# Efficient attention and a Fourier mixing block on one core: five steps set to other places in a hand-written order

## The chip, the cores and the metric

The kernel runs on one core of a Trainium2 chip. Its engines are TensorE (PE in the profile, with PEld for its weight loads), VectorE (DVE), ScalarE (ACT), GpSimd (POOL) and SyncE (SP, which here only issues DMAs). The metric is the device time of one execution in microseconds; a kernel is told by the median of several executions.

## The reference

Eight batches of 576 tokens with 8 heads of 64. Attention is linear: q is softmaxed over its 64 elements, k over the tokens, and q times (k transposed times v) is the result. Its output goes through a two-dimensional Fourier transform whose real part is added, a layer norm, and a feed-forward layer of 2048.

```python
q_s = softmax(q, axis=-1); k_s = softmax(k, axis=2)
kv  = einsum('bhsd,bhse->bhde', k_s, v)
x   = einsum('bhsd,bhde->bhse', q_s, kv)   # to (B, S, H*D)
u   = x + real(fft(fft(x, axis=1), axis=2))
un  = (u - mean(u)) / sqrt(var(u) + 1e-6)
out = u + relu(un @ w_ch1) @ w_ch2
```

## The kernel before

**Groups.** Each batch has 512 tokens of its own group, held as two tiles x of 128 partitions times two rows of 512; the remaining 64 tokens of all eight batches together make a ninth, shared group (xs). Nine groups of 512 tokens go one after the other ("orders" 0 to 8) through the feed-forward layer: groups 0 to 6, then the shared group (number 8), then group 7, the eighth batch.

**One order.** `up` multiplies the normalized and transposed tokens unT with the first weights, `down` the hidden values with the second. Both use Strassen's scheme with seven products in place of eight, with PSUM banks ba, bb and bc; DVE and ACT combine the products (L1141 and L1182 in `up` and in the `down` of order 1, L1304 in the later ones). A bank can't be written by the next product until DVE or ACT has read it. From order 2 on, six of the seven products of `down` are split once more by the same scheme (`deep_down`); the combinations of second weights that this needs are made once, in the `down` of order 1, by `deepen` (L1198): for each of six products two DVE subtractions and two POOL subtractions (L1206) and seven stores of 256 KB to the DRAM buffer w2d (L1212), three of them straight from the streamed weights at once and four from the results six units later. Weights stream from DRAM into four places of the buffer `big`; when the last matmul of a product has used one, `used` (L1194) issues the load of the one four further on (`load`, L449), on SP's queue.

**What else lies in an order.** While PE works on order n, the attention of batch n+1, its transform and its norm are done in between. `attention_timed` (L497) has four key blocks (load L579 and L592, maximum L620 on DVE, Exp L626 on ACT, transposition L644 and L652 on PE, copies L648 and L657, product with v L669) and four query blocks (load L696, maximum L723, Exp L729, transposition L750, product L803 with copy L812 or L814). In every second batch `t_times_kv` (L818) handles the shared tokens: four matmuls (L827), two ACT copies (L834, L835) and three DVE folds (L839 to L842), whose result the transform (`folded`, `block`, from L848 on) takes. `norm` (L996) has four statistics on DVE (L1005, L1006), a Sqrt on ACT (L1009), two small DVE operations (L1012, L1013), four normalizations on ACT (L1034), their transpositions on PE (L1040), copies on ACT (L1048) into unT, and `combine`, three DVE operations and one on POOL (L398 to L401). Its step `back` (L1016) is an Exp of one column on ACT (L1020): it makes the Exp table the active one again after the Sqrt. There is one buffer for unT, which the next group's copies can only fill when the last one has been read.

**The order is written out by hand.** Every step of orders 1 to 8 is a pair of a time and a function. `timed` (L1456) puts the pairs of one order together, they are sorted by time (a stable sort), and their instructions are issued in that sequence to the engines' queues. The times are units without a dimension: one unit is one step of PE in `up`, of four matmul instructions (eight in the `down` of order 1 are two units). So a time tells between which other instructions a step stands in each queue, and nothing more. `up` has 56 units, the `down` of order 1 has 56, the later ones 50. Every queue works its instructions in sequence, also SP's: a DMA that must wait keeps those behind it waiting.

**The stores of group 1** (`down`, function `out` at L1393, and `store`, L1406). Two of the four 256 KB pieces go straight to the output (L1418), two go to a DRAM buffer `mirror` (L1425), from which they are copied to the output with the columns of each head turned around (L1427) nine units later. They stand behind the last additions to x (L1396) on DVE.

Of the kernel before, what the change touches and what calls it, by code (L numbers as in the profile page):

```python
# [80 lines left out]
UP, TWICE = NP * len(ORDER), 8 + 6 * len(ORDER)  # L81
# [12 lines left out]
def at(t, script):  # L94
    return [(t + dt, step) for dt, step in script]
# [42 lines left out]
class _Block:  # L138
# [358 lines left out]
    def attention_timed(self, b, start, end):  # L497

        keys = [("k", b, r) for r in range(NR)]
        tail = [("t", b)] if b % 2 == 0 else []  # L500
        own = [("q", b, c, u) for c in range(2) for u in range(2)]
        first = start + 14 + 5 * len(tail)
        gap, steps = (end - 13.7 - first) / 3, []
        for i, it in enumerate(keys):
            t = start + 3.5 * i
            steps += at(t - 5.5, self.k_load(it)) + at(t, self.k_exp(it)) + at(t + 4, self.k_turn(it))
            steps += at(t + 7, self.k_times_v(it))
        for it in tail:
            t = start + 14
            steps += at(t - 12, self.t_load(it)) + at(t, self.q_exp(it)) + at(t + 8, self.t_turn(it))  # L510
            steps += at(21 if start < 0 else 35, self.t_fold(it))
        for i, it in enumerate(own):
            t = first + gap * i
            steps += at(t - 6.5, self.q_load(it)) + at(t, self.q_exp(it)) + at(t + 8.7, self.q_turn(it))
            steps += at(t + 11.7, self.q_times_kv(it))
        return steps + at((33 if start < 0 else 42) if tail else 22, self.t_times_kv(b))

    def second_keys(self):

# [476 lines left out]
    def norm(self, g):  # L996

        nc, V = self.nc, self.nc.vector
        mv = self.small.tile([P, 4, 2], F32, tag="mv", name="mv", bufs=2)
        std = self.small.tile([P, 4], F32, tag="std", name="std", bufs=2)  # L1000
        uns, box = {}, {}

        def stats(i):
            st = self.small.tile([P, 6], F32, tag="st", name="st", bufs=2)
            V.bn_stats(st[:], self.xpart(g, i % 2, i // 2))  # L1005
            V.bn_aggr(mv[:, i, :], st[:])  # L1006

        def root(s):
            nc.scalar.activation(std[:, s], mv[:, s, 1], ACT.Sqrt, bias=self.eps[:, 0:1])  # L1009

        def scales(s):
            V.reciprocal(std[:, s], std[:, s])  # L1012
            V.scalar_tensor_tensor(out=mv[:, s, 0], in0=mv[:, s, 0], scalar=-1.0, in1=std[:, s], op0=ALU.mult,  # L1013
                                   op1=ALU.mult)

        def back():  # L1016
            if g > 0:

                t = self.small.tile([P, 1], F32, tag="root", name="root", bufs=1)
                nc.scalar.activation(t[:], std[:, 0:1], ACT.Exp, scale=0.0)  # L1020

        def normal(i):
            un = self.halves()
            x = self.xpart(g, i % 2, i // 2)
            if g == 0:
                V.tensor_scalar(out=un[:, 0:D], in0=x, scalar1=std[:, i:i + 1], scalar2=mv[:, i, 0:1], op0=ALU.mult,
                                op1=ALU.add)
                if i == 0:
                    words = self.w2sb.rearrange("p f n -> p (f n)").rearrange("p (a n) -> p a n", n=2 * D)
                    self.gate(un[:], words[0:1, 1:4, 0:2])  # L1030
                if i == 1:
                    self.wait_for(un, [self.raws[i] for i in range(4, 11)])
            else:
                nc.scalar.activation(un[:, 0:D], x, ACT.Identity, bias=mv[:, i, 0:1], scale=std[:, i:i + 1])  # L1034
            uns[i] = un

        def turn(i):
            pt = self.turned()
            for k in range(KT):
                nc.tensor.transpose(pt[:, k, :], uns[i][:, k * P:(k + 1) * P], self.ident[:])  # L1040
            box[i] = pt

        def laid(i):
            if g not in self.unT:
                self.unT[g] = self.work.tile([P, 7, 2, HD], F32, tag="unT", name="unT", bufs=1)
            c, u = i % 2, i // 2
            cols = slice(c * P, (c + 1) * P)
            nc.scalar.copy(self.unT[g][:, u:u + 3:2, :, cols], box.pop(i)[:].rearrange("p (a k) t -> p a k t", a=2))  # L1048

        def combine():  # L1050
            if g > 0:
                unT = self.unT[g]
                self.b_side(lambda i: unT[:, i], lambda i: unT[:, i], V, nc.gpsimd, V)

        steps = []
        put = lambda t, f, *a: steps.append((t, lambda: f(*a)))
        if g == 0:
            for some in ((0, 2), (1, 3)):
                s = slice(some[0], 4, 2)
                for i in some:  # L1060
                    put(0, stats, i)
                for f in (root, scales):
                    put(0, f, s)
        else:
            for n, i in enumerate((0, 2, 1, 3)):
                put((0, 1, 4, 5)[n], stats, i)
            s = slice(0, 4)
            put(6.5, root, s)
            put(9, scales, s)
            put(16.5, back)  # L1070
        for n, i in enumerate((0, 2, 1, 3)):
            put(9.3 + 1.3 * n, normal, i)
            put(11.8 + 1.3 * n, turn, i)
            put(12.6 + 1.3 * n, laid, i)
        put(17.5, combine)
        return steps
# [286 lines left out]
    def down(self, g, order):  # L1363
        if order > 1:
            return self.deep_down(g, order)
        nc, V = self.nc, self.nc.vector
        h = [self.hpairs(p) for p in range(NP)]
        steps, t = [], 4 * 2
        for k, m in enumerate(ORDER):
            if m != 1:  # L1370
                spare = [self.hblock(A_AT[ORDER[k - 1]], a, b) for a in range(2) for b in range(2)]
                n = self.base[order] + NP + k
                steps += at(t * k, self.deepen(m, n, spare if k % 2 else [self.gap(i) for i in range(4)]))

        def product(m, bank, first):
            n = self.base[order] + NP + ORDER.index(m)

            def run(i, q):
                w = self.stream[n]
                for p in range(4 * q, 4 * q + 4):  # L1380
                    nc.tensor.matmul(bank()[:, i, :], lhsT=h[p][:, A_AT[m], i * P:(i + 1) * P], rhs=w[:, p, :],
                                     start=first and i == 0 and p == 0, stop=p == NP - 1,
                                     skip_group_check=True)
                if (i, q) == (1, 1):
                    self.used(n)
            return [lambda i=i, q=q: run(i, q) for i in range(2) for q in range(2)]

        def early(i, j, t):
            u, d = i - 1 if (i, j) != (1, 2) else 0, j - 1
            x = lambda: self.xs[g, u][:, :, d * HD:(d + 1) * HD]  # L1390
            return [(0, lambda: nc.gpsimd.tensor_tensor(out=x(), in0=x(), in1=t()[:], op=ALU.add))]

        def out(u, d, store):  # L1393
            def run(bank, t):
                x = lambda: self.xs[g, u][:, :, d * HD:(d + 1) * HD]
                steps = [(0, lambda: V.tensor_tensor(out=x(), in0=bank()[:], in1=x(), op=ALU.add))]  # L1396
                for c in range(2 * store):
                    steps += at(9 + c, self.store(g, c, u, lambda c=c: self.xpart(g, c, u)))
                return steps
            return run  # L1400


        return steps + self.strassen(product, 2, {(1, 1): out(0, 0, False), (2, 1): out(1, 0, True),
                                                  (2, 2): out(1, 1, False), (1, 2): out(0, 1, True)}, early)
# [26 lines left out]
def kernel(ctx: ExitStack, tc: tile.TileContext, q, kT, v, w1, w2, ft,  # L1431
                                                           cd, out):
    blk = _Block(ctx, tc, q, kT, v, w1, w2, ft, cd, out)
# [22 lines left out]
    def timed(t, order, g):  # L1456
        b = order + 1
        steps = at(t, blk.up(order, g)) + at(t + UP, blk.down(g, order))
        if order == B:
            return steps + [(t + 6 + 1.2 * i, lambda i=i: blk.later and blk.later.pop(0)()) for i in range(36)]  # L1460
        if b == B:
            return steps + at(t + UP + 29, blk.norm(groups[b]))
        start, end = -7 if order > 2 else 0, 45
        steps += at(t, blk.attention_timed(b, start, end)) + at(t + end, blk.folded(b))
        t += UP
# [30 lines left out]
    groups = [*range(B - 1), B, B - 1]  # L1496
# [8 lines left out]
    n = 2 * NF - 10  # L1505
# [20 lines left out]
    n = 0  # L1526
# [15 lines left out]
    t, steps = 0, []  # L1542
    for order, g in enumerate(groups[1:], 1):
        steps += timed(t, order, g)
        t += UP + (TWICE if order > 1 else UP)
# [58 lines left out]
```

## Time and profile before

| | us |
|---|---|
| median of 11 executions | 1115.88 (1113.9 to 1120.67) |
| the profiled execution | 1115.26 |
| its span in the profile | 1113.5 |
| mean granted clock of TensorE | 0.995 |
| `up` of order 1, by the timeline of PE | 193.5 to 257.6 |
| `down` of order 1 | 257.6 to 314.9 |
| `up` of order 2 | 314.9 to 384.1 |
| `down` of order 7 | 961.8 to 1009.8 |

The other busy shares are DVE 60%, POOL 45% and ACT 37%. The hidden layer's matmuls lie on lines L1171 (`up`), L1381 (`down` of order 1), L1267 and L1297 (`deep_down`); in all these rows a tile's name stands before its line, `out<-in`. A line of a timeline has the start, the duration, the engine, the line, the operation with its tiles, how often it occurs, and in brackets the idle time before it with what ended it. A line of the waits has who waited for whom, the total in us, the number of times and the longest.

### The profile page before, as it was taken

How to read it: one execution, taken by the hardware profiler on the slowest of the kernel's cores; microseconds unless marked ns; L12 is line 12 of the kernel's file. 1: busy time of each engine (PE TensorE's matmuls, PEld its weight loads, DVE VectorE, ACT ScalarE, POOL GpSimd, SP SyncE). 2: the span in 40 equal slices, each digit the busy share in tenths (PEclk: the TensorE clock that was granted, in tenths of full speed). 3: DMA queues.
4: the chain of work that ended last, by engine and by line, in shares of the span. 5: the costliest groups of instructions: out<-in, count | busy, mean ns of one | idle time of the engine just before them, and what ended most of it. 6: DMA issues, size and time to landing. Idle time of an engine off the chain costs nothing.

```text
span 1113.5 us, 16988 instructions
## 1 busy us (share of the span) xinstructions
PE 1060.7 (95%) x6336; PEld 917.1 (82%) x6336; DVE 664.1 (60%) x1313; ACT 413.4 (37%) x1001; POOL 498.4 (45%) x409
## 2 busy tenths in 40 slices
PE   5799989999989999999999999999999999999997
PEld 4644446888878899889988998889988998898896
DVE  6784795664646665667555775758456742563351
ACT  6694424452225314442344225521452132222200
POOL 1074671254513545256533841465436353554343
PEclk9999999999999999999999999999999999999999
DMA  9565686446986466636674567466654565575463
GB/s 307 180 225 179 249 293 223 155 156 224 316 284 210 150 235 222 222 142 235 237 259 150 202 242 225 157 223 229 233 201 152 188 239 178 197 264 188 166 238 122
DMA packets 114913, 236.41 MB, mean 212 GB/s; under 512 B 24320, under 2 KB 76288, under 8 KB 104208
## 3 DMA queue, kind: packets, MB, share of 16 engines
q1 hardware_dynamic: 113032, 234.29, 61.0%
q10 hardware_dynamic: 1800, 1.05, 0.3%
q8 instruction: 50, 0.82, 0.3%
q14 instruction: 31, 0.25, 0.1%
HBM read 200.18 MB, written 39.32 MB: 215 GB/s over the span
## 4 chain that ended last, share of the span: by engine, by line
PE 56%; DVE 7%; ACT 2%; issue 1%; DMA 1%; POOL 1%; SPq 0%; DVEq 0%; ACTq 0%; POOLq 0%
PE bb L1171 11%; PE bb L1297 8%; PE bc L1171 7%; PE ba L1171 7%; PE ba L1297 5%; PE bc L1297 5%; PE bb L1267 3%; DVE big L1243 2%; PE acc L669 2%; PE acc L803 1%; PE acc L951 1%; PE tr L1040 1%; PE acc L914 1%; PE acc L917 1%; DVE unT L401 1%
## 5 line engine op out<-in xcount | busy, mean ns | idle before, releaser
L1171 PE MATMUL bb<-unT,big 128*128 128x256 f32 x768 | 185.4, 381 | 8.7 <-DVE krec L631 4.1
L391 POOL TENSOR_TENSOR big<-big 128x512 f32<-128x512 f32 (+1 forms) x38 | 46.3, 1220 | 278.0 <-ACT big L1183 277.2
L1171 PEld LDWEIGHTS bb<-unT,big 128*128 128x128 f32 x768 | 142.8, 191 | 29.1 <-DVE krec L631 4.5
L1183 ACT ACTIVATE big<-big 128x512 f32<-128x512 f32 x96 | 60.4, 629 | 193.0 <-DVE big L1182 192.6
L1171 PE MATMUL ba<-unT,big 128*128 128x256 f32 x512 | 124.1, 379 | 0.2 <-ACT unT L1048 0.2
L1171 PE MATMUL bc<-unT,big 128*128 128x256 f32 x512 | 123.7, 379 | 0.0
L1297 PE MATMUL bb<-big 128*128 128x128 f32 x848 | 105.5, 276 | 3.2 <-DVE u L1304 3.2
L1141 DVE TENSOR_TENSOR u<-bb,s 128x512 f32<-128x512 f32 x66 | 45.5, 689 | 100.0 <-PE bb L1171 87.8
L1171 PEld LDWEIGHTS bc<-unT,big 128*128 128x128 f32 x512 | 94.6, 190 | 12.2 <-DVE big L1182 0.8
L1171 PEld LDWEIGHTS ba<-unT,big 128*128 128x128 f32 x512 | 94.4, 190 | 12.2 <-ACT unT L1048 0.5
L1297 PEld LDWEIGHTS bb<-big 128*128 128x128 f32 x848 | 99.6, 192 | 4.4 <-DVE u L1304 4.4
L1247 POOL TENSOR_TENSOR x<-x,big 128x512 f32<-128x512 f32 x52 | 77.4, 1498 | 35.9 <-DVE big L1304 18.4
L1243 DVE TENSOR_TENSOR big<-big 128x512 f32<-128x512 f32 x92 | 86.1, 979 | 5.9 <-POOL big L392 3.4
L1297 PE MATMUL ba<-big 128*128 128x128 f32 x640 | 79.7, 275 | 0.0
L1297 PEld LDWEIGHTS ba<-big 128*128 128x128 f32 x640 | 76.4, 192 | 1.2
L729 ACT ACTIVATE q<-q,qm 128x64 f32<-128x64 f32 x240 | 64.7, 338 | 30.8 <-DVE qm L723 23.8
L1243 POOL TENSOR_TENSOR big<-big 128x512 f32<-128x512 f32 x26 | 41.4, 1604 | 61.5 <-DVE big L1243 61.5
L1182 DVE TENSOR_TENSOR big<-bc,u 128x512 f32<-128x512 f32 x64 | 44.0, 688 | 23.6 <-PE bc L1171 22.5
L1304 DVE TENSOR_TENSOR u<-bb,s 128x256 f32<-128x256 f32 x40 | 16.8, 419 | 63.5 <-PE bb L1297 45.6
L1297 PE MATMUL bc<-big 128*128 128x128 f32 x416 | 51.7, 275 | 0.0
L1267 PE MATMUL bb<-big 128*128 128x256 f32 x224 | 51.5, 381 | 0.0
L392 POOL TENSOR_TENSOR big<-big 128x512 f32<-128x512 f32 (+1 forms) x38 | 47.9, 1261 | 2.5
(281 smaller groups left out, 2048.8 us busy)
## 6 DMA issues: line engine op xcount, KB each, us to landing
big<-w2d SPq DMA_DIRECT2D x67, 1024.0 KB
big<-w1s SPq DMA_DIRECT2D x64, 896.0 KB
big<-w2s SPq DMA_DIRECT2D x16, 1024.0 KB
big<-in_w_dram SPq DMA_DIRECT2D x21, 512.0 KB
w2d<-big SPq DMA_DIRECT2D x42, 256.0 KB
q<-in_q_dram SPq DMA_DIRECT2D x27, 256.0 KB
k<-in_kT_dram SPq DMA_DIRECT2D x24, 288.0 KB
v<-in_v_dram SPq DMA_DIRECT2D x24, 256.0 KB
```

Of the source, the lines that this page charges most:

```text
L391: e1.tensor_tensor(out=to(4), in0=at(2), in1=at(3), op=ALU.add)
L392: e1.tensor_tensor(out=to(2), in0=at(0), in1=at(2), op=ALU.subtract)
L669: nc.tensor.matmul(pk, lhsT=ks[:, c, :], rhs=v[:, c, :], start=(c == 0), stop=(c == NC - 1))
L729: nc.scalar.activation(q[:, h, :], q[:, h, :], ACT.Exp, bias=m[:, h:h + 1])
L1141: plus = lambda t: V.tensor_tensor(out=temp(t), in0=box["bb"][:], in1=box["s1"][:], op=ALU.add)
L1171: nc.tensor.matmul(bank()[:, i, :], lhsT=w[:, WA_AT[m], k * P:(k + 1) * P], rhs=self.unT[g][:, B_AT[m], k, :], start=first and i == 0 and ...
L1182: steps = [(0, lambda: V.tensor_tensor(out=hp(i), in0=bank()[:], in1=u()[:], op=ALU.add)), (0.8, lambda: nc.scalar.activation(hp(i), hp(i) ...
L1183: (0.8, lambda: nc.scalar.activation(hp(i), hp(i), ACT.Relu))]
L1243: e.tensor_tensor(out=to(o), in0=to(x), in1=to(y), op=op)
L1247: G.tensor_tensor(out=x, in0=x, in1=tile(m), op=ALU.add)
L1267: nc.tensor.matmul(box[name][:, i, :], lhsT=h[p][:, A_AT[m], i * P:(i + 1) * P], rhs=self.stream[n][:, p, :], start=i == 0 and p == 0, sto ...
L1297: nc.tensor.matmul(box[place[n]][:, i, :], lhsT=own(m)(A_AT[n])[:, f, :], rhs=w[:, r // 2, r % 2 * P:r % 2 * P + P], start=first and f == ...
```

## The change

Five numbers in the written order are changed, nothing else: the same instructions work on the same data.

```diff
@@ attention_timed
-        return steps + at((33 if start < 0 else 42) if tail else 22, self.t_times_kv(b))
+        return steps + at((33 if start < 0 else 39) if tail else 22, self.t_times_kv(b))
@@ norm
-            put(16.5, back)
+            put(13.6, back)
@@ down (order 1)
-                steps += at(t * k, self.deepen(m, n, spare if k % 2 else [self.gap(i) for i in range(4)]))
+                steps += at(t * k - 4 * (k % 2 == 0), self.deepen(m, n, spare if k % 2 else [self.gap(i) for i in range(4)]))
@@ down (order 1), out
-                    steps += at(9 + c, self.store(g, c, u, lambda c=c: self.xpart(g, c, u)))
+                    steps += at(15 + c, self.store(g, c, u, lambda c=c: self.xpart(g, c, u)))
@@ timed, order 7
-            return steps + at(t + UP + 29, blk.norm(groups[b]))
+            return steps + at(t + UP + 14, blk.norm(groups[b]))
```

- `t_times_kv`: `start` is 0 only in orders 1 and 2, and only batches with an even number have shared tokens to handle, so this concerns order 1 (batch 2): its shared tokens stand three units earlier.
- `back`: in the seven norms of orders 1 to 7 the Exp that brings the table back stands after the last normalization and before the second of the four copies into unT, no longer before the last. The norm of group 1 takes its steps by their number in the list and stays as it is.
- `deepen`: the second, fourth and sixth combination start at units 12, 28 and 44 of the `down` of order 1 in place of 16, 32 and 48; the others stay at 8, 24 and 40.
- stores of group 1: six units later, so all lie in the `up` of order 2: the first two at its units 6.5 and 7.5 (0.5 and 1.5 before), the other two at 14.5 and 15.5 (8.5 and 9.5 before), and the turned copies nine units after their pieces.
- norm of the eighth group: starts at unit 14 of the `down` of order 7 in place of 29; all its steps, table and combination included, move with it.

## The prediction

> **What bounds the kernel now.** I read the page's first part, then the waits of PE, then the timeline of PE around each wait, then the engine that ended it.
>
> ```profile
> PE 1060.7 (95%) x6336; PEld 917.1 (82%) x6336; DVE 664.1 (60%) x1313; ACT 413.4 (37%) x1001; POOL 498.4 (45%) x409
> ...
> PE bb L1171 <- DVE krec L631: 4.1, 1, 4.1
> PE bb L1171 <- DVE u L1141: 3.3, 2, 1.8
> ...
> PE bb L1171 <- DVE big L1304: 1.2, 2, 0.6
> ```
>
> PE is busy all through, so an edit is worth something only where it closes a hole in PE. After 170 us the timeline of PE has 20.2 us of holes, 19.7 of them in holes over 0.25 us. Those near the edited steps: 1.83 at 250.6, 4.11 at 330.0, 1.22 four times (442.0, 559.6, 677.7, 796.6), 0.61 at 915.1 and at 1012.3. Their sum, 12.0 us, bounds the gain, but for the clock.
>
> The longest hole, in the timelines of PE, DVE and SP, and in the windows (columns: busy us of PE, PEld, DVE, ACT, POOL, then PEclk, DMA share, GB/s):
>
> ```profile
> 329.99 1.59 PE L1171 MATMUL bb<-unT,big 128*128 128x256 f32 x4 [4.11 <-DVE krec L631]
> ...
> 328.46 0.76 DVE L620 TENSOR_REDUCE km<-k 128x1 f32<-128x576 f32 x1 [7.93 <-DMA k<-in_kT_dram]
> 329.25 0.69 DVE L1141 TENSOR_TENSOR u<-bb,s 128x512 f32<-128x512 f32 x1
> ...
> 319.73 0.32 SPq L449 DMA_DIRECT2D big<-w1s  x1
> 320.10 0.43 SPq L1425 DMA_DIRECT2D mirror<-x  x1
> 320.56 0.43 SPq L1418 DMA_DIRECT2D out_dram<-x  x1
> 321.09 0.45 SPq L579 DMA_DIRECT2D k<-in_kT_dram  x1
> ...
> 280.00:328.00 48.00, 45.88 (x231) 40.27 (x229) 23.97 (x44) 10.10 (x18) 18.06 (x13) 1.00 1.03 335
> 330.50:333.90 3.40, 3.40 (x14) 3.14 (x14) 1.72 (x5) 2.21 (x5) 0.00 (x0) 0.50 0.00 0
> ```
>
> The reader is to see a chain. DVE stands on the maximum of the third key block (L620) for 7.93 us, because its load, issued at 321.09, lands only near 328.4. Behind it in DVE's queue is L1141, which would free PE's bank bb. The load is late because the DMA engines are full (335 GB/s, share 1.03) with the combinations' stores, a weight load and two output stores. And the hole costs more than its length: for the next 3.4 us the granted clock is 0.50.
>
> [...] 4.11 us idle, then 0.50 for 3.4 us; holes of 1.83 us and less are followed by 1.00. [...] L449 at 319.73 could not be issued while SP stood from 317.4 on for w2d stores, and the later loads stood behind it. [...] L839 takes 1.44 us beside POOL and 0.49 alone.
>
> **Part 1: shared tokens of the second group, unit 42 to 39 (L516).**
>
> ```profile
> 245.99 1.44 DVE L839 SCALAR_TENSOR_TENSOR eo<-eo,sign 128x255 f32<-128x255 f32 x1
> 247.47 1.24 DVE L841 TENSOR_TENSOR eo<-eo 128x128 f32<-128x128 f32 x1
> 248.74 1.23 DVE L842 TENSOR_TENSOR eo<-eo 128x128 f32<-128x128 f32 x1
> 249.90 0.68 DVE L1141 TENSOR_TENSOR u<-bb,s 128x512 f32<-128x512 f32 x1
> ```
>
> PE has finished bank bb at 247.1, but L1141 stands behind three folds (3.9 us) until 249.90, and PE waits 1.83 us. DVE is idle for 2.82 us before 245.39. Three units earlier the matmuls (1.05 us) come at about 239.5 in place of 242.5; their input F is ready at 238.4. The two ACT copies (0.57 and 0.58) follow to about 241.8; the folds start at 242.6 and, still beside POOL, last to 246.5. L812 slips from 245.4 to 246.5; L1141 runs from about 247.2 to 247.9, before PE wants the bank at 248.8. So -1.83. Ends: 0.5 us of it remains if the folds start a us later (-1.3); more than the hole cannot be gained.
>
> **Part 2: even combinations four units earlier (L1373), stores six later (L1398).** Three combinations move, each of 2 DVE (0.68), 2 POOL (1.30) and 7 stores of 256 KB. PE never waits in this stage and DVE has idle stretches (8.7 us before 277.7), so their arithmetic costs nothing; its inputs are weights whose loads go out more than 10 us earlier. What counts is SP. Today each weight load of L449 in 284 to 320 stands on SP behind combinations just issued, and waits for some of their stores: the product ends on PE at 299.5, 307.7 and 315.0, the loads go out at 303.7, 311.8 and 319.7. Moved, the even stores lie half a product ahead and the last load can go out at about 315.2. There is also a stretch near 279 and one near 304 in which SP waits and little moves; the earlier stores fill them, so the backlog ends earlier, not only in another order.
>
> The load of the third key block then waits only for PE's last transposition of the first (319.9) and goes out at 320.0, with neither the 896 KB load freshly in front of it nor the two stores of 256 KB. I estimate its landing at 322.5. It must land by 324.4: 0.76 for L620 and 0.69 for L1141 end at 325.9, where PE stops today. So the hole goes, -4.11, and with it 3.4 us at half clock, -1.70. Ends: nothing if the landing stays; -5.81. Late next are the fourth key block (its maximum stands before a bank that PE wants at about 332) and the first query load, which now has two stores before it on SP (0.86 us of issue): needed by about 335, I estimate it at 329.5. The two later stores and the mirrored rows go out among loads that have 5 us and more.
>
> **Part 3: Exp table (L1070), in seven norms.** L1020 (0.20 us, 1.28 with its load) moves ahead of the second to fourth copies L1048.
>
> ```profile
> 909.19 0.37 ACT L1318 COPY big<-ba 128x256 f32<-128x256 f32 x1 [1.64 <-PE ba L1297]
> 909.58 1.28 ACT L1020 ACT_TABLE_LOAD   x1
> 910.87 0.20 ACT L1020 ACTIVATE root<-std 128x1 f32<-128x1 f32 x1
> 910.98 0.57 ACT L1048 COPY unT<-tr 128x512 f32<-128x512 f32 x1
> ```
>
> Here the last copy is ready but waits 1.4 us; behind it DVE's three operations L398 to L401 (3.0 us) and L1304, for which PE waits 0.61 at 915.1. Moved, the load lies at about 904.8 to 906.0, when the second copy slips by 0.6 and PE's fourth transposition (907.7) still finds its buffer free. DVE ends L401 at 913.3: -0.61. In the four orders with attention the load already comes before (with L626); only about 0.10 us of L1020 leaves the chain that ends in the 1.22 us holes: -0.4. In order 1 the last copy waits for PE anyway: 0. Ends for the part: -0.3 and -1.2.
>
> **Part 4: the eighth group's norm, fifteen units earlier (L1462).** It takes along 4 statistics (0.68 and 0.18 each), the Sqrt load and root (1.28, 0.30), two small DVE operations (0.17 each), 4 normalizations (0.80), 16 transpositions, 4 copies (0.59), L1020, three DVE combinations (3.0) and one on POOL (1.77); no DMA. At the end of order 7 this frees DVE: the hole at 1012.3 goes, -0.61 (part 3 alone would do that too). The price is at 976 to 984, where DVE is tight: two statistics (1.7 us) come before L1304, which today runs 977.92 to 978.34 and must end by 979.5. I place it at 979.2 to 979.6: +0.2. The next banks have 0.6 us or more. The unT buffer is read until about 983, the first copy into it comes near 987. Ends: -0.6 and +1.0.
>
> **Sum.** -1.83 - 5.81 - 1.01 - 0.41 = -9.1 us. The profiled execution took 1115.26 us (span 1113.5 and 1.8 around it), so 1106.2; the median, 1115.88, lies 0.6 higher, so I forecast 1106.8.
>
> **Rivals.** (A) The forecast, 1106.8; own range 1105.2 to 1108.3.
> (B) The key load lands at 325 to 327: the stores leave its way, but the backlog does not shrink. For it: the same bytes pass through engines that are full. Against: SP's stretches of waiting vanish. The hole shrinks to about 1.7 us and the clock holds, so 1.7 less is gained: 1108.5.
> (C) The hole stays over 3.4 us, since transfer and not order bounds it: only parts 1, 3 and 4 are left, -3.3: 1112.6.
> (D) Slower: the first query load of order 2 becomes the new stop. It is in DVE's queue before the L1141 that frees bb. Each us by which it lands after about 335 is a us of PE[...]. If the backlog is as in C and the two stores push this load to 344, that is +9 and +1.7 against -3.3: about 1122. Break-even is a landing at about 338. Against: it goes out near 326 and the bytes before it take some 4 us at 335 GB/s.
>
> **How the numbers follow.** A 0.60, B 0.20, C 0.12, D 0.08. A change under 0.2% (2.2 us) can't be told from none here. Faster: A, B and 0.07 of C, 0.87; within: 0.05 of C; slower: D, 0.08. The range 1105.2 to 1111.5 holds A and B with their ends and leaves out C and D.
>
> **What would show it.** The clock row at 0.50 near 330 gone and L620 there not waiting for a DMA over 3 us: part 2. No wait of L1171 for L1141 near 249: part 1. No table load before the last L1048 of a norm: part 3. No wait for L1304 of 0.61 at the starts of the last two orders, at most 0.3 us of a new one after 979: part 4. Wrong it is if a hole of over 3.4 us stands anywhere after 200 us.

## The result and the profile after

The changed kernel takes 1107.54 us (median of 12 executions, 1105.96 to 1110.78) against 1115.86 for the kernel before (47 executions); the ratio is 0.9927, with a 95% interval of 0.9917 to 0.9938. That is 8.3 us of the 9.1 that were forecast. The profiled execution took 1107.6 us, with a span of 1105.8.

The waits of PE in the changed kernel (who waited for whom: us in total, times, longest):

```profile
PE acc L669 <- ACT ks L648: 13.5, 12, 3.6
...
PE bb L1171 <- DVE krec L631: 1.5, 1, 1.5
PE bb L1171 <- DVE u L1141: 1.5, 1, 1.5
```

The hole of PE behind the third key block's maximum is 1.5 us in place of 4.1. One of the two waits for L1141 is gone (1.83); the other, of 1.50 in order 2, no edit touched. The wait for L1304 at the starts of the last two orders is not in the list any more. The timeline of DVE in the changed kernel, first at the hole of order 1 that is gone, then where the longest hole was:

```profile
245.33 0.47 DVE L839 SCALAR_TENSOR_TENSOR eo<-eo,sign 128x255 f32<-128x255 f32 x1
245.84 0.29 DVE L841 TENSOR_TENSOR eo<-eo 128x128 f32<-128x128 f32 x1
246.17 1.41 DVE L842 TENSOR_TENSOR eo<-eo 128x128 f32<-128x128 f32 x1
247.50 0.68 DVE L812 TENSOR_TENSOR x<-acc,qrec 128x512 f32<-128x512 f32 x1
249.14 0.69 DVE L1141 TENSOR_TENSOR u<-bb,s 128x512 f32<-128x512 f32 x1 [0.96 <-PE bb L1171]
```

```profile
320.13 0.29 DVE L657 COPY ks<-tr 64x128 f32<-64x128 f32 x1
325.77 0.75 DVE L620 TENSOR_REDUCE km<-k 128x1 f32<-128x576 f32 x1 [5.34 <-DMA k<-in_kT_dram]
326.55 0.69 DVE L1141 TENSOR_TENSOR u<-bb,s 128x512 f32<-128x512 f32 x1
```

In order 1, L1141 now waits for PE and no longer PE for it. In order 2, DVE still stands on the key block, for 5.34 us, and L1141 still stands behind it; but the load has landed 2.7 us earlier. SP in the same kernel:

```profile
312.77 0.81 SPq L449 DMA_DIRECT2D big<-w1s  x1
313.68 2.59 SPq L1212 DMA_DIRECT2D w2d<-big  x4
316.36 0.55 SPq L449 DMA_DIRECT2D big<-w1s  x1
319.86 0.33 SPq L579 DMA_DIRECT2D k<-in_kT_dram  x1
```

The key load goes out at 319.86, as soon as its buffer is free, and no store of group 1 stands before it. But four stores of 256 KB and a weight load went out only from 313.7 on. In the trace the parts of that weight load landed from 323.27 to 324.99 and those of the key load from 324.00 to 325.74, so the two were still under way side by side. The windows of the changed kernel (busy us of PE, PEld, DVE, ACT, POOL; PEclk, DMA share, GB/s) show that the DMA engines stay full (share 1.01), and that the clock holds after the hole (1.00 from 328.0 on):

```profile
280.00:328.00 48.00, 46.48 (x233) 40.84 (x232) 24.36 (x47) 11.18 (x21) 14.82 (x10) 1.00 1.01 315
328.00:331.40 3.40, 3.40 (x24) 3.14 (x24) 2.39 (x9) 2.47 (x6) 0.00 (x0) 1.00 0.70 251
```

**Where the time went.** From the first matmul of order 1 to the end the two profiled executions take 919.97 and 910.33 us, 9.64 less. The holes of PE shrink by 7.03: 1.83 (part 1), 2.59 (part 2), four times 0.09 and 0.61 (part 3), 0.61 (order 8), and 1.02 in order 5, in a stage that no edit touches (last section). The half clock of 3.4 us near 330 was worth another 1.7. So 7.7 us are accounted for by the edits. The rest, 0.9, is in no hole of PE; 0.3 of it lies after the last matmul (from 1106.67 to 1113.47 before, from 1099.30 to 1105.79 after). What lies before order 1 took 1.95 us longer in the changed kernel's profile, with 6.8 us at half clock near 32 us which the other execution has not.

### The profile page after: what moved, and what is told of

Same layout as the page of the kernel before. It is cut to its first block, busy times and chain, and to the rows that moved or that the text cites. A ratio compares the mean times of both kernels' runs of the same rounds, so it can differ in the third digit from the quotient of the medians.

```text
span 1105.8 us, 16987 instructions
## 1 busy us (share of the span) xinstructions
PE 1059.9 (96%) x6336; PEld 917.0 (83%) x6336; DVE 662.6 (60%) x1313; ACT 412.5 (37%) x1001; POOL 498.7 (45%) x409
## 4 chain that ended last, share of the span: by engine, by line
PE 59%; DVE 6%; ACT 1%; issue 1%; POOL 1%; DVEq 0%; ACTq 0%; POOLq 0%
PE bb L1171 11%; PE bb L1297 8%; PE bc L1171 7%; PE ba L1171 7%; PE ba L1297 5%; PE bc L1297 5%; PE bb L1267 4%; DVE big L1243 2%; PE acc L669 2%; PE acc L803 1%; PE acc L914 1%; PE acc L917 1%; PE acc L951 1%; PE tr L1040 1%; PE tr L750 1%
## 5 line engine op out<-in xcount | busy, mean ns | idle before, releaser
L1141 DVE TENSOR_TENSOR u<-bb,s 128x512 f32<-128x512 f32 x66 | 45.5, 690 | 100.6 <-PE bb L1171 90.8
L1247 POOL TENSOR_TENSOR x<-x,big 128x512 f32<-128x512 f32 x52 | 81.3, 1573 | 35.9 <-DVE big L1304 18.4
L1304 DVE TENSOR_TENSOR u<-bb,s 128x256 f32<-128x256 f32 x40 | 16.7, 419 | 65.2 <-PE bb L1297 50.2
```

Of the source, the lines that this page charges most:

```text
L1141: plus = lambda t: V.tensor_tensor(out=temp(t), in0=box["bb"][:], in1=box["s1"][:], op=ALU.add)
L1247: G.tensor_tensor(out=x, in0=x, in1=tile(m), op=ALU.add)
```

## The experiments

Each edit was first made alone in the kernel before. A number such as 0.9995 is the ratio of its times to those of the kernel before, with the 95% interval behind it.

**e1_tokens: the shared tokens alone.**

```diff
-        return steps + at((33 if start < 0 else 42) if tail else 22, self.t_times_kv(b))
+        return steps + at((33 if start < 0 else 39) if tail else 22, self.t_times_kv(b))
```

> The kernel before with the shared tokens of batch 2 at unit 39 alone. Theory (the three folds on DVE kept L1141 from freeing bank bb): the 1.83 us hole of PE near 250.6 goes, nothing opens in its place, ratio to before about 0.9984 (-1.8 us of 1115.9); the 4.11 us hole near 330 and its 3.4 us at half clock stay. Rival (the transform of batch 2 is what is late, and the folds only stand in front of it): the hole comes back as a wait for L858 to L880 or for the first transform matmul L914, ratio 1.000.

Measured: 0.9995 (0.9985 to 1.0006). The hole at 250.6 is gone and nothing stands in its place. Still the median gains only 0.7 us and the interval holds 1.000, so the ratio can't tell this edit from none; only the profile shows what it does. The profile shows one reason for the spread: near 330 its hole was 4.28 us, and the clock then stayed at half for 6.8 us, twice as long as in the kernel before. PE still stood for 0.7 us of that, so a hole of nearly the same length cost some 1.4 us more.

**e2_combinations and e3_stores: the two halves of part 2.**

```diff
-                steps += at(t * k, self.deepen(
+                steps += at(t * k - 4 * (k % 2 == 0), self.deepen(
```

> The kernel before with the even combinations four units earlier alone; the stores of group 1 stay in front of the third key block's load. Theory (the key load is late because of the bytes in front of it, and the two stores of 256 KB are some 1.5 us of these at 335 GB/s): L449 goes out earlier than 319.7 after its counterpart's shift, the key load lands about 1.5 us later than in the changed kernel, so the hole is about 3.0 us in place of 1.52 and 4.11; the clock holds or not[...]: ratio 0.9975 to 0.9990. Rival 1 (the stores alone make the load late): hole 4.1, half clock, ratio 1.000. Rival 2 (the combinations alone make it late): hole 1.5 or less and no half clock, ratio 0.9961.

```diff
-                    steps += at(9 + c, self.store(g, c, u, lambda c=c: self.xpart(g, c, u)))
+                    steps += at(15 + c, self.store(g, c, u, lambda c=c: self.xpart(g, c, u)))
```

> The kernel before with the stores of group 1 six units later alone. Theory (bytes in front of the key load): its issue comes about 1 us earlier and 512 KB no longer stand in front, it lands some 1.5 to 2.4 us earlier, hole 1.7 to 2.6, clock holds: gain 1.5 to 2.4 plus 1.7, ratio 0.9963 to 0.9971. Rival 1 (the combinations' backlog alone makes it late): hole 4.1 and half clock, ratio 1.000. Rival 2 (the two parts overlap: either removes the whole of what both remove): hole 1.5, ratio 0.9961, and the combinations alone give the same.

Measured: the combinations alone 0.9990 (0.9976 to 1.0003), with executions from 1110.65 to 1120.03; the stores alone 0.9956 (0.9943 to 0.9970). PE and SP with the combinations alone, then PE with the stores alone:

```profile
332.74 1.22 PE L1171 MATMUL bb<-unT,big 128*128 128x256 f32 x2 [6.44 <-DVE krec L631]
```

```profile
316.65 0.81 SPq L449 DMA_DIRECT2D big<-w1s  x1
317.55 2.66 SPq L1212 DMA_DIRECT2D w2d<-big  x4
320.31 0.53 SPq L449 DMA_DIRECT2D big<-w1s  x1
320.93 0.77 SPq L1425 DMA_DIRECT2D mirror<-x  x1
321.75 0.69 SPq L1418 DMA_DIRECT2D out_dram<-x  x1
324.53 0.33 SPq L579 DMA_DIRECT2D k<-in_kT_dram  x1
```

```profile
327.23 1.13 PE L1171 MATMUL bb<-unT,big 128*128 128x256 f32 x4 [1.06 <-DVE krec L631]
```

The combinations alone did not meet their expectation, a hole of about 3.0 us: it grew to 6.44 in this execution, which is one of the slower half of them. The weight loads are issued at 316.65 and 320.31, where the kernel before has 311.78 and 319.73, and the key load goes out at 324.53 in place of 321.09. From there to L620 it took 6.7 us, less than the 7.4 before: it was late because it was issued late. After the last store SP stood for 2.0 us before it. The profile names a transposition of the second key block for this wait, but in the kernel before the same load goes out ahead of that transposition. What SP waited for in these 2.0 us was not shown.

The stores alone leave a hole of 1.06, less than was expected (1.7 to 2.6), with no half clock after it (mean of its profile 0.998): all that part 2 brought is theirs.

**e4_exp_table: the Exp table alone.**

```diff
-            put(16.5, back)
+            put(13.6, back)
```

> The kernel before with the step that brings the Exp table back at 13.6 alone. Theory: no table load before the last L1048 of any norm; the holes of 0.61 us at the starts of the last two orders go, the four of 1.22 become about 1.12: -1.6 us, ratio 0.9986. Rival (the second copy, now behind the table load, makes PE's fourth transposition wait): new waits of L1040 for ACT in the norms, up to 0.6 each, ratio 0.9990 to 1.002.

Measured: 0.9982 (0.9974 to 0.9991). ACT in the norm at the end of order 6:

```profile
904.83 0.82 ACT L1034 ACTIVATE eo<-xs,mv,std 128x512 f32<-128x512 f32 x1
905.65 1.28 ACT L1020 ACT_TABLE_LOAD   x1
906.94 0.20 ACT L1020 ACTIVATE root<-std 128x1 f32<-128x1 f32 x1
907.05 0.57 ACT L1048 COPY unT<-tr 128x512 f32<-128x512 f32 x1
907.84 0.59 ACT L1048 COPY unT<-tr 128x512 f32<-128x512 f32 x1 [0.22 <-PE tr L1040]
910.06 0.37 ACT L1318 COPY big<-ba 128x256 f32<-128x256 f32 x1 [1.64 <-PE ba L1297]
910.33 0.59 ACT L1048 COPY unT<-tr 128x512 f32<-128x512 f32 x1
```

The load lies behind the last normalization, where the third copy waits for PE anyway, and the last copy follows L1318 at once. Both holes of 0.61 are gone and the four before L669 are 1.12, as expected.

**e5_norm8 and e9_no_norm8: the eighth norm alone, and all but it.**

```diff
-            return steps + at(t + UP + 29, blk.norm(groups[b]))
+            return steps + at(t + UP + 14, blk.norm(groups[b]))
```

> The kernel before with the norm of the eighth batch at unit 14 of order 7 alone. Theory: the hole of 0.61 us at the start of order 8 (1012.3) goes, the one at the start of order 7 stays, and DVE's statistics cost PE at most 0.3 us near 979: -0.3 to -0.6 us, which is too little to be told from the median; read from the holes. Rival (DVE is too tight in units 14 to 20): new waits of L1297 for DVE L1304 of 0.6 us or more between 976 and 990.

> The changed kernel with the norm of the eighth batch back at unit 29. Theory: the Exp table's new place alone already closes the hole of 0.61 us at the start of order 8, so part 4 adds nothing beside part 3: no hole there and no difference to the changed kernel, ratio 0.9915 to 0.994. Rival (the prediction's small cost, or a gain of its own): a hole of 0.3 us or more in order 7 that the changed kernel has not, or the reverse.

Measured: alone 0.9986 (0.9977 to 0.9994); all but it 0.9943 (0.9924 to 0.9962), a little above the range that was expected; its interval overlaps the changed kernel's. Alone it takes the hole at the start of order 8 and leaves that of order 7. Without it, but with the table's new place, there is no hole at the start of order 8 either. Nor is there a new one in order 7 in any kernel with this edit. So it adds nothing beside part 3 that a hole shows; the 1.5 us by which its median alone is lower are more than the 0.61 that the profile accounts for. The execution of e9 tells something else (PE, then a window):

```profile
327.06 1.50 PE L1171 MATMUL bb<-unT,big 128*128 128x256 f32 x4 [2.45 <-DVE krec L631]
```

```profile
327.70:331.10 3.40, 3.40 (x15) 3.12 (x14) 1.58 (x5) 2.07 (x5) 0.00 (x0) 0.50 0.26 97
```

Up to order 7 this kernel is the changed one, so this shows how much one and the same sequence varies between executions: the key load went out at 318.69 and took 6.8 us to L620, where the changed kernel's profile has 5.9; the hole was 2.45 us in place of 1.52, and 3.4 us at half clock followed it.

**e6_no_combinations: the changed kernel with the combinations where they were.** The edit is the line of e2 reversed.

> The changed kernel with the even combinations back at 16, 32, 48. Theory after the first four runs (the order on SP decides: bytes issued ahead of the third key block's load; the two stores are all that matters, the earlier combinations only put weight loads later on SP): hole near 327 about 1.1 us, no half clock there, ratio 0.991 to 0.9935, not slower than the changed kernel at 0.9927. Rival (the prediction's: the earlier combinations shrink the backlog and are part of the gain): hole over 1.5 us, ratio over 0.9935.

Measured: 0.9927 (0.9905 to 0.9948), the same as with them, and a hole of 1.38 (1.52 with them), the clock at full there (mean of its profile 0.998); the profiled execution, 1105.17, is the fastest of six that reach up to 1112.40. Beside the moved stores the combinations' place makes no difference that can be told in the ratio. The holes, with the stores moved, are 1.06 (e3) and 1.38 (e6) with the combinations at their old place, 1.52 and 2.45 (e9) with them earlier: if anything, that edit harms, but two profiles each don't show it.

**e7_keys_alone: the order in DVE's queue itself.** The kernel before, with one edit that is not in the change: the arithmetic of the third and fourth key block of order 2 comes two units later, the loads stay.

```diff
-            steps += at(t - 5.5, self.k_load(it)) + at(t, self.k_exp(it)) + at(t + 4, self.k_turn(it))
+            steps += at(t - 5.5, self.k_load(it))
+            t += 2 * (b == 3 and i > 1)
+            steps += at(t, self.k_exp(it)) + at(t + 4, self.k_turn(it))
             steps += at(t + 7, self.k_times_v(it))
```

> The kernel before, and in order 2 the maxima, transpositions and products of the third and fourth key block two units later; their loads, the stores and the combinations stay where they were. The load lands as late as before, near 328.4. Theory (the hole is the sequence in DVE's queue: L1141, whose data were there at 322.4, stands behind a maximum that waits for a DMA): L1141 goes at 322.4, PE does not stop at 325.9, hole gone or under 1 us (then at the key block's transposition), no half clock: ratio 0.9945 to 0.996. Rival (the late load itself bounds the stage): PE stops a little later for the transposition or the product of that block for 3 us or more, ratio over 0.998.

Measured: 0.9943 (0.9928 to 0.9958). The timeline of DVE in this kernel (lines are two higher here: L1143 is L1141, L622 is L620):

```profile
323.17 0.69 DVE L1143 TENSOR_TENSOR u<-bb,s 128x512 f32<-128x512 f32 x1 [2.00 <-PE bb L1173]
...
325.70 0.29 DVE L659 COPY ks<-tr 64x128 f32<-64x128 f32 x1 [0.50 <-PE tr L654]
328.73 0.75 DVE L622 TENSOR_REDUCE km<-k 128x1 f32<-128x576 f32 x1 [2.73 <-DMA k<-in_kT_dram]
```

The key block's maximum still waits until 328.73, as late as in the kernel before (328.46). But L1141 goes as soon as PE is ready, PE has no hole near 330, and the clock holds (mean of its profile 0.996, before 0.995). So it was not the landing as such that stopped PE before, but the place of L1141 behind the instruction that waits for it.

**e8_best, e10_keys_and_all and e11_queries: this edit on top.** e8 is the changed kernel with the combinations back and the edit of e7; e10 has all five edits of the change and that of e7; e11 is e8 with the third and fourth query block of order 2 moved too:

```diff
-            t = first + gap * i
+            t = first + gap * i + (0, 0, 0.6, 0.25)[i] * (b == 3)
```

> The changed kernel with the even combinations back at 16, 32, 48 and with the two key blocks of order 2 two units later. Theory: no hole at 327 (1.1 to 1.5 us less than the changed kernel), ratio 0.990 to 0.992. Rival (PE finds the next stop as soon as this one goes, such as the product L669 or the query maximum): a new hole of about 1 us before 345, ratio 0.9925 to 0.9935.

> The changed kernel, all five edits, with the third and fourth key block's arithmetic of order 2 two units later. Theory: the even combinations neither help nor harm once DVE does not stand before L1141; hole at 327 gone, ratio 0.989 to 0.992, like the kernel with the combinations back in their places (0.990). Rival (the earlier combinations let the key load land late enough to stop the transposition too): a hole for L644 or L669 before 335, ratio over 0.992.

> The kernel of ratio 0.990 with the third and fourth query block of order 2 0.6 and 0.25 units later, so that L1141 at unit 31.5 stands before the sums of the third and the maximum of the fourth on DVE. Theory (the same sequence in DVE's queue makes the 1.50 us hole near 355): the hole goes, ratio about 0.9887. Rival (DVE is simply full there): the hole moves to the next bank or to a transposition L750, ratio 0.990.

Measured: e8 0.9900 (0.9882 to 0.9917), 1105.45 us; e10 0.9916 (0.9902 to 0.9930), 1106.28 us; e11 0.9903 (0.9887 to 0.9919), 1105.22 us. In none is there a hole between 320 and 340. In e11 the hole of 1.50 became one of 0.80 before the transposition L750, a little later, at the place that its rival named, though only half of its length; 0.7 us is too little for the ratio. All three lie below the changed kernel's 0.9927; e8's interval just touches its interval, the others' overlap it.

## Why the prediction held, and where it did not

- **The time**: 1107.54 lies in the range and near the 1106.8; the direction was right. That it came so near is in part luck: in the profiles the edits account for 7.7 us, not 9.1, and the medians lie 0.6 us further apart than the two profiled executions do.
- **Part 1** was sized at -1.83, and its hole is gone in the changed kernel and in e1. The working was off in detail: two of the three folds ran before POOL's next work (0.47 and 0.29 us) and only L842 beside it (1.41), so L1141 was not late at all. In the ratio of the edit alone it did not show.
- **Part 2** is the term that was mis-sized: -5.81 was forecast, and its hole gave 2.59 and the clock 1.70, together -4.3. The step that failed is "so the backlog ends earlier, not only in another order" with the landing at 322.5: the load went out at 319.86, as forecast (320.0), but it landed only at about 325.7. The weight load in front of it, forecast to go out at 315.2, went out at 316.36, and its last part landed at 324.99. That it went out earlier gained nothing: in e3, where it goes out 0.5 us ahead of the key load, the landing is no later (325.70). This is rival B for this step. The clock row at half is gone, as the forecast had it; "L620 there not waiting for a DMA over 3 us" is not so (5.34). And of its two halves the stores carry the gain (e3, e6); with the combinations alone the hole grew in the profile (e2), so the reason that the forecast gave for moving them did not hold.
- **Part 3**: -1.01 forecast; the hole at 915 and 0.09 from each of four others make 0.97. It also closes the hole at 1012, which the text named as possible.
- **Part 4**: -0.41 forecast with +0.2 for a new stop near 979. The stop did not come: L1304 began at 972.42, 3.64 us after the one before it at 968.78 (2.56 in the kernel before), and its bank was read in time. Beside part 3 the edit's own part is nothing (e9).
- **The rivals** C and D did not come. D's own terms, +9 and +1.7 against -3.3, add up to about 1123, not 1122. The forecast's last sign looks for a hole of over 3.4 us; in e9 one of 2.45 us already had a stretch at half clock (0.50 for 3.4 us) behind it.

## What to carry to other kernels

An engine's queue was here the place where a late transfer stopped work that has nothing to do with it (4.11 us of PE before): look for what stands behind the waiting instruction, and move that in front before speeding up the transfer (e7, at 0.9943, needs none of the five edits for the largest part of their gain). Where the transfer engines are full (share 1.03 here), moving transfers that stand before an urgent one behind it helped (e3, 0.9956); moving others among themselves did not create room here, and the urgent one went out later (e2, 324.53 in place of 321.09). A table load on ACT (1.28 us) belongs where the next instruction waits for another engine anyway (e4, 0.9982).

## What was not expected of the hardware

- In these profiles the clock after a hole of PE does not follow from the length of the hole alone. Near 330, behind the third key block's maximum, 4.11 us in the kernel before, 4.31 in e4 and 2.45 in e9 were followed by 3.4 us at half clock; 4.28 in e1 were followed by 6.8, of which PE still stood for 0.7. In e2, where the hole of 6.44 ended at 332.74, the clock was 0.50 from 331.2 to 338.0, and PE stood for 1.5 us of that. After 1.52 in the changed kernel (327.30), and after 1.83 (250.63) and 1.50 (362.13) in the kernel before, it stayed at 1.00. What decides between 3.4 and 6.8 us was not shown; that a hole of 2.45 us would have half clock behind it was not foreseen.
- Before order 1 the profiled executions differ by 4.9 us (the first matmul of `up` at 193.43 to 198.34), with 0, 3.4, 6.8 or 13.6 us at half clock before 40 us. Between there and the end, what is left after the holes over 0.15 us and half of the time that PE worked at half clock is 896.9 to 899.4 us in all thirteen profiles.
- The hole of 1.02 us near 750 in order 5 is there in three of thirteen profiles (the kernel before, e3, e7). Before it DVE waits 4.36 and 1.70 us for two key loads (L585) that kept SP for 1.10 and 0.71 us at their issue; in the changed kernel, without the hole, the waits are 3.39 and 1.74 us and the issues 0.42 and 0.46. With one profile of each kernel it is open whether the hole belongs to a kernel or to an execution; the cause was not looked for.
